# Batch 0 of an FNet and GLU kernel: the even slots of its sequence transform mixed by s mod 4 and summed over half the columns, the second weight piece merged last

## The chip, the cores and the metric

One Trainium2 chip, of which the kernel uses one core. The metric is the device time of one execution in microseconds: 1909.48 us, the median of three runs of the kernel before (1908.13 to 1910.03). The profile is one further execution of it.

## What is computed

The input x has 8 batches of 3008 rows of 256 numbers. Each batch goes through a Fourier transform over the rows and over the 256 features, of which the real part is kept; then every row goes through a gated feed-forward network (FFN).

```
X = np.fft.fft(x, axis=1); X = np.fft.fft(X, axis=2); x = X.real      # 8 x 3008 x 256
gate = 1 / (1 + exp(-(x @ w_gate)))                                   # 256 -> 1536
out  = (gate * (x @ w_val)) @ w_out                                   # 1536 -> 256
```

x is float32, the weights are float64.

## The kernel before

**Feature transform.** It is never computed on the data. Each piece of 256 columns of w_gate and w_val is multiplied by a small table `dt` (`merge`, L410: four matmuls into one PSUM bank, two copies on ScalarE into G2 and G1, two small DMAs into `ge`). A weight piece first has to be turned from float64 to float32: `weight_parts` (L377, two ScalarE instructions, L382 and L383), `weight_join` (L385, three VectorE instructions, L392 to L395, and one GpSimd addition, L397). Pieces are numbered by `jobs`: 0 is w_gate's first 256 columns, 1 is w_val's first, 2 and 3 the second ones, and so on. `weight_use(j)` calls `merge`. Below, "join j" and "merge j" are these steps of piece j.

**Sequence transform of batch 0.** The rows s = 0 to 767 stand as s = 6 p + q, partition p and slot q = 0 to 5, and with each come its mirror rows (3008 - s, 1504 + s, 1504 - s). VectorE folds these four (`half_rows`, L571, lines L494 to L583) into sums W for even frequencies (blk 0) and odd ones (blk 1). The folds go by `SLICES`: slots 0 and 1, slots 2 and 3, slot 4, slot 5. TensorE then multiplies the folds with the tables ST[0] (cosine) and ST[1] (sine), six slots each with 377 columns for even frequencies and 376 for odd ones. Even slots add up in one PSUM bank (`ev`), odd slots in another (`od`), because the first sum is symmetric and the second antisymmetric about the middle frequency: `places` (L611) makes the low frequencies from their sum (L613) and the high ones from their difference (L617), into pk (cosine) and qk (sine). These are 24 products of 377 or 376 columns, in four groups (two frequency blocks, cosine and sine).

**The e group.** One feature (number 128) has its own sums, twelve matmuls with one column of weights against the cosine table (`e_sums`, L696, tile `pe`), then copies on ScalarE (L720, L721, L726) and `places` on VectorE into `er`. The first 252 of them are copied into `e0`, which the FFN's first five groups multiply by G2; the whole is stored to DRAM (`ed`, L733), from where later groups get it as rows `ek` (`e_rows`, L760), with which ScalarE fills (seeds) their PSUM banks (L772).

**Order.** The whole program is an order written by hand; each engine runs its instructions in that order. SP issues all loads in program order: first weight pieces 0 and 1, then rows and tables slot by slot, then the other weight pieces. After both first merges come folds and products, then the FFN in 576 steps i: for each of 8 batches 6 chunks of up to 252 frequencies, for each chunk 12 groups of 128 hidden features. Step i issues `front_a(i)` (pk times G1), ScalarE's doubling `part(i)` (L787), the gate of group i - 1 (sigmoids L801 and L815, VectorE L802, L814, L818), `front_b(i)` (qk times G2), and from i = 5 on the output product of group i - 5. In steps 0 to 12 the remaining pieces are joined and merged, `weight_use(2)` in step 0 and 3 and 5 in step 1. Three PSUM banks (tag x) go round for `pf`, the FFN's sums; five others (po0 to po4) are for outputs and, earlier, for transforms.

**Side work.** `at(i, f)` hangs work on step i. For batch 1 rows are rearranged through DRAM (`xr`, L155 to L168), table rows are reversed into `rtab` (L206), and at steps 17 and 18 sixteen quarter loads (L247) refill the place of ST[1] for the later batches. At steps 21 to 27 seven `e_load`s follow (L685), columns of 4 bytes for feature 128 of the other batches, whose sums (`e_joint`, step 40) use ST[0] as batch 0 had it. The tables that later batches use are made at steps 42 on.

Of the kernel before, what the change touches and what calls it, by code (L numbers as in the profile page):

```python
# [8 lines left out]
F32 = mybir.dt.float32  # L9
# [72 lines left out]
def kernel(  # L82
# [107 lines left out]

    def load_rows(q, n):
        nc.sync.dma_start(out=X[0][0:NP, :, q : q + n], in_=xf[0, :, :, q : q + n])  # L192

    def load_table(t, q, n, lo=0, hi=NE + NO):
        nc.sync.dma_start(out=ST[t][0:NP, q : q + n, lo:hi], in_=stab[:, t, q : q + n, lo:hi])

# [206 lines left out]
    def weight_use(j):  # L403
        w, c = jobs[j]
        if w == 2:
            WO[c] = WS.pop(j)
        else:
            merge(WS.pop(j), w, c, (4, 2, 3)[next(turns) % 3] if j > 1 else None)

    def merge(ws, g, c, other):  # L410
        cs = slice(c * WC, (c + 1) * WC)
        ps = bank("ps", other)
# [71 lines left out]

    SLICES = ((0, 1), (2, 3), (4,), (5,))

    def fold_ops(b, nq):
# [83 lines left out]
        else:  # L571

            def half_rows(q):
# [9 lines left out]
                nc.vector.memset(r[:, :, :, 0:1], 0.0)  # L583
            ops += [lambda q=q: half_rows(slice(q[0], q[-1] + 1)) for q in SLICES]
        for blk, (v, r) in enumerate(parts):
# [8 lines left out]

    def half(b, w, d, blk, sn, other=None):


        c0, n = ((0, NE), (NE, NO))[blk]
        ev, od = [bank(name, other and other[i])[:, 0:n] for i, name in enumerate(("ev", "od"))]

        def sums(*qs):
            for q in sorted(qs, key=lambda q: q % 2):
                mm((ev, od)[q % 2], w(q), ST[int(sn)][0:NP, q, c0 : c0 + n], q < 2, q >= NQ - 2)

        def then():
            a = evp.tile([P, NE], F32, name="a", tag="a")[:, 0:n]
            nc.scalar.copy(a, ev)
            return lambda: places(d, blk, sn, a, od)
        return sums, then

# [68 lines left out]

    def seq_group(b, blk, what, other=None):  # L680
        return half(b, lambda q: W[b, blk][what][:, q, :], PQE[b][what], blk, what == 1, other)


    def e_load(b):
# [11 lines left out]
    def e_sums(m=B - 1):  # L696


        ps = bank("pe", NB - 1)
        at_ = lambda blk, par: slice((2 * blk + par) * TB, (2 * blk + par) * TB + m)  # L700
# [253 lines left out]
    load_x(0)  # L954
    for j in range(2):
        weight_load(j)
    load_rows(0, 2)
    load_table(0, 0, 2)
    load_rows(2, 2)
    load_table(1, 0, 2, 0, NE)  # L960
    load_table(0, 2, 2)
    load_rows(4, 1)
    load_table(0, 4, 1)
    load_rows(5, 1)
    weight_load(2)
    load_table(1, 2, 2, 0, NE)
    load_table(0, 5, 1)
    load_table(1, 4, 2, 0, NE)
    load_table(1, 0, NQ, NE)
    for j in (3, 5, 6, 8, 9, 4, 7):  # L970
        weight_load(j)
# [3 lines left out]
    weight_parts(0)  # L975
    weight_parts(1)
    weight_join(0)
    weight_join(1)
# [5 lines left out]
    seq_start(0)  # L984

    cos = [seq_group(0, blk, 0, (2 * blk, 2 * blk + 1)) for blk in range(2)]
    e_, e_even = e_sums(1)
    sin = [seq_group(0, 0, 1)]
    for q, f in zip(SLICES, fold_ops(0, 2), strict=True):
        f()  # L990
        e_(*{1: (0, 1), 5: (2, 3, 4, 5)}.get(q[-1], ()))
        sin[0][0](*{5: (3,)}.get(q[-1], ()))
        cos[0][0](*q)
        cos[1][0](*q)
        sin[0][0](*{1: (0, 1), 4: (2,), 5: (4, 5)}.get(q[-1], ()))
    places_c = [cos[blk][1]() for blk in range(2)]
    weight_parts(2)
    weight_join(2)
    rest, *ends = e_even()
    rest()  # L1000
    for f in ends:
        f()
    for f in places_c:
        f()
    nc.scalar.copy(e0[0:1], E0[0][:, 0:CH])
    weight_parts(3)
    weight_join(3)
    sin.append(seq_group(0, 1, 1, (0, 1)))
    sin[1][0](*range(NQ))
    for j in range(KEEP, KEEP + 3):  # L1010
        weight_load(j)
    places_s = [group[1]() for group in sin]
    for f in places_s:
        f()
    e_rows(0)
# [4 lines left out]
    def at(i, *fs):  # L1020
        side.setdefault(i, []).extend(fs)
# [21 lines left out]
    for i, f in zip((1, 2, 2, 2, 3, 4, 4, 4, 5, 6, 6, 8, 8, 8, 9, 9, 9, 9, 10, 10, 10, 11, 11), quarter_x(1), strict=True):  # L1043
        at(i, f)
    at(i0 + 1, lambda: load_x(1))
    for b in range(1, B):
        at(20 + b, lambda b=b: e_load(b))
# [198 lines left out]
```

## Time and profile before

| | |
|---|---|
| median of three runs | 1909.48 us |
| the profiled execution | 1909.15 us |
| its span, first to last instruction | 1907.4 us |
| TensorE busy | 1895.6 us, 99% |
| VectorE, ScalarE, GpSimd busy | 80%, 71%, 81% |
| granted TensorE clock | 1.00 throughout |
| first fold's last instruction | 15.40 us |
| ScalarE's first copy of batch 0's e sums starts | 26.18 us |
| first FFN matmul's weights loaded | 32.73 us |
| DMA, first 40 us | 290, 380, 381, 340 GB/s in tens of us |

In the lines of the profile, PE is TensorE's matmul, PEld its weight load, DVE VectorE, ACT ScalarE, POOL GpSimd, SPq the queue of SyncE that issues DMAs. A row of the timeline has the start in us, the duration in us, engine, line, operation, output and inputs, and in brackets how long the engine was idle before and what released it. A row of waits has who waited for whom, the total in us, how often, and the longest. A float32 matmul shows as two records. A row of the chain has start and duration of a piece of what ended last. A row of the stretches has a window, its length, the busy time (and instruction count) of PE, PEld, DVE, ACT and POOL, the clock, the DMA engines' busy share and GB/s.

### The profile page before, as it was taken

Reading aid. Unit: us, or ns where it says so; the run is one execution under the profiler, and the core shown is the slowest. Engines: PE = TensorE matmul, PEld = TensorE weight load, DVE = VectorE, ACT = ScalarE, POOL = GpSimd, SP = SyncE. Lnnn points to the kernel's source line nnn. Section 1 sums busy time; section 2 is a strip of 40 time slices with the busy share of each in tenths; the row PEclk is TensorE's granted clock in tenths of the full one; section 3 lists DMA queues with packets and bytes.
Section 4 is the critical chain, followed back from the end, with each engine's and each line's share of the span. In section 5 each row is a group of like instructions: output and inputs, shape, how many; then the busy total and the mean of one; then the engine's idle time right before and its main releaser. Section 6 shows DMA issues by size and latency. Waiting matters only on the chain.

```text
span 1907.4 us, 36057 instructions
## 1 busy us (share of the span) xinstructions
PE 1895.6 (99%) x11836; PEld 1756.6 (92%) x11836; DVE 1520.6 (80%) x3375; ACT 1353.2 (71%) x3235; POOL 1543.4 (81%) x2733
## 2 busy tenths in 40 slices
PE   8999999999999999999999999999999999999999
PEld 5788999999999999999999999999999999999998
DVE  7678888878979778897788878888788777977775
ACT  4777777777777777777777777677767777777775
POOL 2489879987999779997799878999789986877770
PEclk9999999999999999999999999999999999999999
DMA  8446221212022121211211212122120110010001
GB/s 315 120 134 80 71 89 51 72 33 81 21 64 54 31 87 32 62 41 37 89 39 48 45 39 81 40 52 58 30 74 17 36 37 15 15 25 17 15 18 30
DMA packets 197333, 109.33 MB, mean 57 GB/s; under 512 B 134823, under 2 KB 188818, under 8 KB 195354
## 3 DMA queue, kind: packets, MB, share of 16 engines
q1 hardware_dynamic: 196568, 106.50, 21.1%
q8 instruction: 95, 1.56, 0.3%
q14 instruction: 92, 0.75, 0.1%
q10 hardware_dynamic: 546, 0.51, 0.1%
q0 software_dynamic: 32, 0.00, 0.0%
HBM read 71.24 MB, written 47.87 MB: 62 GB/s over the span
## 4 chain that ended last, share of the span: by engine, by line
PE 94%; DMA 2%; SPq 1%; POOL 1%; ACT 1%; DVE 0%; issue 0%; ACTq 0%; POOLq 0%
PE pf L133 49%; PE po L133 41%; PE sum L133 2%; DMA rtab<-in_stab_dram 1%; PE ps L133 1%; POOL sf L824 1%; DMA st<-in_stab_dram 1%; SPq L206 1%; DMA raw<-in_moe_w_val_dram 0%; PE od L133 0%; POOL x L507 0%; SPq L192 0%; SPq L375 0%; PE pe L133 0%; PE ev L133 0%
## 5 line engine op out<-in xcount | busy, mean ns | idle before, releaser
L824 POOL TENSOR_TENSOR sf<-h,sf 128x168 f32<-128x168 f32 (+1 forms) x1104 | 621.0, 582 | 79.5 <-DVE h L818 75.9
L824 POOL TENSOR_TENSOR sf<-h 128x168 f32<-128x168 f32 (+1 forms) x920 | 519.3, 584 | 159.8 <-DVE h L818 158.0
L133 PE MATMUL pf<-qk,G 128*128 128x252 f32 (+1 forms) x2304 | 583.4, 376 | 0.9 <-ACT ae L787 0.8
L133 PE MATMUL pf<-pk,G 128*128 128x252 f32 (+1 forms) x2304 | 582.7, 376 | 0.0
L772 ACT ACTIVATE pf<-ek,ge 128x252 f32<-128x252 f32 (+1 forms) x1142 | 538.2, 471 | 23.2 <-DMA ge<-G 3.0
L133 PE MATMUL po<-sf,wf 128*128 128x168 f32 (+1 forms) x2944 | 508.3, 305 | 0.0
L787 ACT ACTIVATE ae<-pf 128x504 f32<-128x504 f32 (+1 forms) x576 | 338.8, 588 | 218.7 <-PE pf L133 217.2
L133 PEld LDWEIGHTS pf<-pk,G 128*128 128x128 f32 x2304 | 435.9, 190 | 53.3 <-ACT pf L772 1.5
L133 PE MATMUL po<-h,wf 128*128 128x168 f32 (+2 forms) x2584 | 461.3, 307 | 0.0
L133 PEld LDWEIGHTS po<-sf,wf 128*128 128x128 f32 x2944 | 453.4, 190 | 8.0
L818 DVE TENSOR_TENSOR h<-pf,z 128x252 f32<-128x252 f32 (+1 forms) x576 | 240.4, 417 | 274.0 <-ACT pf L815 270.5
L802 DVE TENSOR_TENSOR z<-ae,pf 128x504 f32<-128x504 f32 (+1 forms) x576 | 384.6, 668 | 83.1 <-ACT h L801 79.1
L908 DVE TENSOR_TENSOR c<-c 128x168 f32<-128x168 f32 (+1 forms) x920 | 438.7, 500 | 3.3
L133 PEld LDWEIGHTS pf<-qk,G 128*128 128x128 f32 x2304 | 410.6, 190 | 32.3 <-ACT ae L787 2.1
L133 PEld LDWEIGHTS po<-h,wf 128*128 128x128 f32 x2584 | 410.4, 190 | 17.8 <-issue 0.9
L801 ACT ACTIVATE h<-pf 128x252 f32<-128x252 f32 (+1 forms) x576 | 216.9, 376 | 146.3 <-PE pf L133 129.0
L815 ACT ACTIVATE pf<-z 128x252 f32<-128x252 f32 (+1 forms) x576 | 214.3, 372 | 116.4 <-DVE h L814 114.5
L814 DVE TENSOR_TENSOR h<-h,pf 128x252 f32<-128x252 f32 (+1 forms) x576 | 232.9, 404 | 0.0
L824 POOL TENSOR_TENSOR sf<-sf 128x168 f32<-128x168 f32 (+1 forms) x184 | 101.7, 553 | 14.4
L824 POOL TENSOR_TENSOR sf<-sf,h 128x168 f32<-128x168 f32 (+1 forms) x184 | 110.1, 598 | 0.0
L891 ACT COPY c<-po 128x504 f32<-128x504 f32 (+1 forms) x138 | 78.5, 569 | 0.0
L918 DVE STREAM_TRANSPOSE os<-c 128x256 f32<-128x256 f32 x188 | 76.5, 427 | 0.1
(158 smaller groups left out, 876.4 us busy)
## 6 DMA issues: line engine op xcount, KB each, us to landing
x<-xr SPq DMA_DIRECT2D x14, 1536.0 KB
out_dram<-os SPq DMA_DIRECT2D x376, 56.0 KB
xr<-in_xf_dram SPq DMA_DIRECT2D x105, 128.0 KB
x<-x SPq DMA_DIRECT2D x112, 96.0 KB
xr<-in_xf_dram SPq DMA_DIRECT2D x14, 384.0 KB
ek<-ed SPq DMA_DIRECT2D x40, 126.0 KB
out_dram<-os SPq DMA_DIRECT2D x288, 7.0 KB
xr<-in_xf_dram SPq DMA_DIRECT2D x21, 124.0 KB
```

What stands on the lines that cost most here:

```text
L133: nc.tensor.matmul(o, l, r, start=start, stop=stop, skip_group_check=True)
L772: nc.scalar.activation(PF[i][:, g], EK[i // NFT], AF.Copy, scale=ge[:, g, f : f + 1])
L787: nc.scalar.activation(AP[i], PF[i], AF.Copy, scale=2.0)
L801: nc.scalar.activation(H[p][:, fh, 0:n], PF[i][:, 0], AF.Sigmoid)
L802: nc.vector.tensor_tensor(z[:, :, ::-1], AP.pop(i), PF[i], op=ALU.subtract)
L814: nc.vector.tensor_tensor(h[:, fh, 0:n], h[:, fh, 0:n], pf[:, 1], op=ALU.mult)
L815: nc.scalar.activation(pf[:, 0], z[:, 0], AF.Sigmoid)
L818: nc.vector.tensor_tensor(h[:, fh, n:], pf[:, 0], z[:, 1], op=ALU.mult)
L824: nc.gpsimd.tensor_tensor(block(p, dst), block(p, a), block(p, b), op=(ALU.subtract, ALU.add)[op])
L891: (nc.vector.tensor_copy if t == 1 or t == 3 else nc.scalar.copy)(C[0][:, 3 * t * R : 3 * (t + 1) * R], PO[t][:, 0 : 3 * R])
L908: nc.vector.tensor_tensor(t[:, dst * R : (dst + 1) * R], *v, op=(ALU.subtract, ALU.add)[op])
L918: nc.vector.transpose(os_[0][0][:, s, 0:nb, h, :], t[:, c0 : c0 + nb * TB])
```

## The change

It concerns batch 0 and its loads, and adds two loads later.

- In slots 0 and 2 the even partitions and the odd partitions are exchanged between the two slots at loading (`mixed`), for rows and tables, so that slot 0 holds rows s = 0 mod 4 and slot 2 rows s = 2 mod 4. The sums of each have a symmetry of their own about the quarter frequency, so that only columns H0 to H1 (188 to 565, the upper half of the even frequencies and the lower half of the odd ones) are multiplied, into banks x and y.
- Slot 4 is not mixed at loading; its two kinds stand on alternate partitions. Its half columns are loaded into four tiles `apart` with zeros on the other kind's partitions (GpSimd memsets), so that its products are four, two for each bank.
- `copy` (ScalarE) and `join` (two VectorE instructions) make the full row of 753 even-slot sums from x and y; `places` then works from that row and the `od` banks.
- Order: rows and tables 1 and 3 are loaded first, weight piece 1 after rows 5; the cosine table's other columns of slots 0 and 2, in eight loads to alternate partitions, and slot 4 whole come after both slots 5, for the e group. `SLICES` becomes (1, 3), (0, 2), 4, 5. Merge 1 stands behind the e group; VectorE, not ScalarE, copies e0; the combinations for low frequencies (`pk(blk, 0)`, `qk(blk, 0)`) come first and those for high ones last, around the joins of pieces 2 and 3. The bank of the e group is one of the three of tag x.
- At step 20, `load_again` loads slots 0 and 2 of the cosine table unmixed, for `e_joint`.

```diff
+    def mixed(q):
+        return ((slice(0, NP, 2), q), (slice(1, NP, 2), 2 - q)) if q in (0, 2) else ((slice(0, NP), q),)
+    def load_rows(*qs):
+        for q in qs:
+            for ps, r in mixed(q):
+                nc.sync.dma_start(out=X[0][ps, :, q], in_=xf[0, ps, :, r])
+    H0, H1 = NE // 2, NE + NO // 2
+    def load_table(t, q, lo=0, hi=NE + NO):
+        for ps, r in mixed(q):
+            nc.sync.dma_start(out=ST[t][ps, q, lo:hi], in_=stab[ps, t, r, lo:hi])
+    apart = [[wf[:, 2 * t + h].rearrange("p m n -> p (m n)")[:, 6 * WC : 6 * WC + NE] for h in range(2)]
+             for t in range(2)]
+    def load_apart(t):
+        for h in range(2):
+            nc.sync.dma_start(out=apart[t][h][h:NP:2], in_=stab[h::2, t, 4, H0:H1])
+    def load_again():
+        for q in (0, 2):
+            nc.sync.dma_start(out=ST[0][0:NP, q], in_=stab[:, 0, q])
...
-            merge(WS.pop(j), w, c, (4, 2, 3)[next(turns) % 3] if j > 1 else None)
+            merge(WS.pop(j), w, c, HELD.pop(j) if j in HELD else bank("ps", 2 + next(turns) % 3 if j else None))
...
-    SLICES = ((0, 1), (2, 3), (4,), (5,))
+    SLICES = (slice(1, 4, 2), slice(0, 3, 2), slice(4, 5), slice(5, 6))
...
+    def seq_sums(what, x, y, od):
...
+        cols = (H0, NE - H0, 0), (NE, NO // 2, NE - H0)
+        def even(*qs):
+            for q in qs:
+                for blk, (lo, n, to) in enumerate(cols):
+                    for h in range(2):
+                        if q == 4 or h == q // 2:
+                            tab = apart[what][h][0:NP, to : to + n] if q == 4 else ST[what][0:NP, q, lo : lo + n]
+                            mm((x, y)[h][:, to : to + n], w[blk][:, q], tab, q != 4 and blk == 0, q == 4)
+        def odd(blk, *qs):
+            lo, n = ((0, NE), (NE, NO))[blk]
+            for q in qs:
+                mm(od[blk][:, 0:n], w[blk][:, q], ST[what][0:NP, q, lo : lo + n], q == 1, q == NQ - 1)
+        def copy():
+            a = evp.tile([P, NE], F32, name="a", tag="a")
+            nc.scalar.copy(a, y[:, 0:NE])
+            return a
+        def join(a):
+            f = hp.tile([P, 6 * WC], F32, name="u", tag="h") if what else wf[:, 0].rearrange("p m n -> p (m n)")
+            nc.vector.tensor_tensor(f[:, H0:H1], x[:, 0:NE], a, op=ALU.add)
...
+            nc.vector.tensor_tensor(f[:, 0 : 2 * H1].rearrange("p (b n) -> p b n", b=2)[:, :, H0 - 1 :: -1], *two,
+                                    op=ALU.subtract)
+            return lambda blk, *ends: places(d, blk, what == 1, f[:, blk * NE : NE + blk * NO],
+                                             od[blk][:, 0 : NE - blk], ends)
...
-        ps = bank("pe", NB - 1)
+        ps = bank("pe", NB - 1 if m > 1 else None)
...
+    for t in apart:
+        for tab in t:
+            nc.gpsimd.memset(tab, 0.0)
+    weight_load(0)
+    load_rows(1, 3)
+    for q in (1, 3):
+        load_table(0, q)
     load_rows(0, 2)
+    for q in (1, 3):
+        load_table(1, q)
+    load_rows(4)
+    for q in (0, 2):
+        load_table(0, q, H0, H1)
+    load_apart(0)
+    load_rows(5)
+    for q in (0, 2):
+        load_table(1, q, H0, H1)
+    load_apart(1)
+    weight_load(1)
+    for t in range(2):
+        load_table(t, 5)
+    for q in (0, 2):
+        load_table(0, q, 0, H0)
+        load_table(0, q, H1)
+    load_table(0, 4)
+    for j in (2, 3, 5, 6, 8, 9, 4, 7):
         weight_load(j)
...
+    next(folds)()
+    odd(0, 1, 3)
+    odd(1, 1, 3)
+    odd_s(0, 1, 3)
+    e_(1, 3)
+    next(folds)()
+    even(0, 2)
+    next(folds)()
+    even(4)
+    a = copy()
+    next(folds)()
+    pk = join(a)
+    HELD[1] = bank("ps")
+    od_s.append(bank("od"))
+    even_s(0, 2)
+    odd_s(1, 1, 3)
+    even_s(4)
+    odd(0, 5)
+    odd(1, 5)
+    weight_parts(1)
+    a = copy_s()
+    weight_join(1)
+    for blk in range(2):
+        pk(blk, 0)
+    qk = join_s(a)
+    odd_s(0, 5)
+    e_(0, 2, 4, 5)
+    qk(0, 0)
+    rest, last, end = e_even()
+    rest()
     weight_use(1)
+    odd_s(1, 5)
+    last()
+    nc.vector.tensor_copy(e0[0:1], E0[0][:, 0:CH])
     weight_parts(2)
+    qk(1, 0)
     weight_join(2)
+    qk(1, 1)
     weight_parts(3)
     weight_join(3)
+    for blk in range(2):
+        pk(blk, 1)
+    qk(0, 1)
+    end()
     for j in range(KEEP, KEEP + 3):
         weight_load(j)
...
+    at(20, load_again)
```

More of the change, by code (lines that the diff above doesn't have):

```diff
@@ L189 @@
     ed = dram.tile([B, NK + 1], F32, name="ed")
[L191 to L195, printed above, removed]
+    def mixed(q):
[16 more added lines that the diff above has]
+            nc.sync.dma_start(out=ST[0][0:NP, q], in_=stab[:, 0, q])
     NQ4 = NE // 4 + 1
@@ L407, in weight_use, with merge @@
         else:
-            merge(WS.pop(j), w, c, (4, 2, 3)[next(turns) % 3] if j > 1 else None)
-    def merge(ws, g, c, other):
+            merge(WS.pop(j), w, c, HELD.pop(j) if j in HELD else bank("ps", 2 + next(turns) % 3 if j else None))
+    HELD = {}
+    def merge(ws, g, c, ps):
         cs = slice(c * WC, (c + 1) * WC)
-        ps = bank("ps", other)
         for h in range(2):
@@ L583, in half_rows @@
                 nc.vector.memset(r[:, :, :, 0:1], 0.0)
-            ops += [lambda q=q: half_rows(slice(q[0], q[-1] + 1)) for q in SLICES]
+            ops += [lambda q=q: half_rows(q) for q in SLICES]
         for blk, (v, r) in enumerate(parts):
@@ L593 @@
     PQE = {}
[L595 to L609, printed above, removed]
+    def seq_sums(what, x, y, od):
+        d = PQE[0][what]
+        w = [W[0, blk][what] for blk in range(2)]
+        cols = (H0, NE - H0, 0), (NE, NO // 2, NE - H0)
[17 more added lines that the diff above has]
+            nc.vector.tensor_tensor(f[:, H0:H1], x[:, 0:NE], a, op=ALU.add)
+            two = [t[:, 1:NE].rearrange("p (b n) -> p b n", b=2) for t in (x, a)]
+            if what:
+                two.reverse()
+            nc.vector.tensor_tensor(f[:, 0 : 2 * H1].rearrange("p (b n) -> p b n", b=2)[:, :, H0 - 1 :: -1], *two,
+                                    op=ALU.subtract)
+            return lambda blk, *ends: places(d, blk, what == 1, f[:, blk * NE : NE + blk * NO],
+                                             od[blk][:, 0 : NE - blk], ends)
+        return even, odd, copy, join
     def places(d, blk, sn, ev, od, ends=(0, 1)):
@@ L678, in seq_start @@
             nc.vector.memset(t[:, NK:], 0.0)
-    def seq_group(b, blk, what, other=None):
-        return half(b, lambda q: W[b, blk][what][:, q, :], PQE[b][what], blk, what == 1, other)
     def e_load(b):
@@ L954 @@
     load_x(0)
-    for j in range(2):
-        weight_load(j)
-    load_rows(0, 2)
[L958 to L970, printed above, removed]
+    for t in apart:
[5 more added lines that the diff above has]
+        load_table(0, q)
+    load_rows(0, 2)
+    for q in (1, 3):
[16 more added lines that the diff above has]
+    for j in (2, 3, 5, 6, 8, 9, 4, 7):
         weight_load(j)
@@ L975 @@
     weight_parts(0)
-    weight_parts(1)
     weight_join(0)
-    weight_join(1)
     warm = bank("warm", 2)
@@ L982 @@
     weight_use(0)
-    weight_use(1)
[L984 to L996, printed above, removed]
+    seq_start(0)
+    folds = iter(fold_ops(0, 2))
+    even, odd, copy, join = seq_sums(0, bank("u"), bank("u"), [bank("od", t) for t in range(2)])
+    e_, e_even = e_sums(1)
+    od_s = [bank("od", 4)]
+    even_s, odd_s, copy_s, join_s = seq_sums(1, bank("u", 2), bank("u", 3), od_s)
+    next(folds)()
[28 more added lines that the diff above has]
+    rest()
+    weight_use(1)
+    odd_s(1, 5)
+    last()
+    nc.vector.tensor_copy(e0[0:1], E0[0][:, 0:CH])
     weight_parts(2)
+    qk(1, 0)
     weight_join(2)
[L999 to L1005, printed above, removed]
+    qk(1, 1)
     weight_parts(3)
     weight_join(3)
-    sin.append(seq_group(0, 1, 1, (0, 1)))
-    sin[1][0](*range(NQ))
+    for blk in range(2):
+        pk(blk, 1)
+    qk(0, 1)
+    end()
     for j in range(KEEP, KEEP + 3):
         weight_load(j)
-    places_s = [group[1]() for group in sin]
-    for f in places_s:
-        f()
     e_rows(0)
```

## The prediction

> **What bounds the kernel now.** I read the busy shares first, then the waits of TensorE, then the chain that ended last, piece by piece over the first 160 us, and then each engine's rows in order of time there. The first line says that TensorE is busy almost from end to end; the next three are all that it waits for after its first 6 us.
>
> ```profile
> PE 1895.6 (99%) x11836; PEld 1756.6 (92%) x11836; DVE 1520.6 (80%) x3375; ACT 1353.2 (71%) x3235; POOL 1543.4 (81%) x2733
> ...
> PE ps L133 <- POOL raw L397: 1.6, 1, 1.6
> PE pf L133 <- ACT ae L787: 0.8, 2, 0.6
> PE ev L133 <- DVE x L583: 0.2, 1, 0.2
> ```
>
> So from about 33 us on, where the FFN's first matmuls begin, the time is TensorE's own work, which the diff leaves alone. What can change is when that stream starts, whether it then runs without holes, and two added transfers near 146 us. The chain shows what sets the start: transfers until 23.7 us, then TensorE alone.
>
> ```profile
> 14.43 9.31 DMA st<-in_stab_dram
> 23.74 0.04 issue
> 23.78 0.90 PE ev L133 x2
> 24.68 1.37 PE pe L133 x16
> ...
> 33.21 4.25 PE pf L133 x20
> ```
>
> The stretches give the transfer rate that my sum uses: 2.9 MB in the first 10 us, then 0.38 MB/us (last column, GB/s).
>
> ```profile
> 0.00:10.00 10.00, 4.21 (x13) 3.50 (x14) 3.64 (x6) 3.94 (x6) 2.80 (x8) 1.00 0.83 290
> 10.00:20.00 10.00, 8.19 (x34) 4.58 (x33) 9.72 (x18) 1.29 (x4) 2.15 (x1) 1.00 1.04 380
> 20.00:30.00 10.00, 9.90 (x43) 4.92 (x42) 8.20 (x23) 3.91 (x8) 1.28 (x1) 1.00 1.06 381
> ```
>
> Check: up to cosine slot 5 the old order moves 8.07 MB, due at 10 + 5.17/0.38 = 23.6 us; it landed at 23.7.
>
> **Transfers, part by part.** Sizes: a row slot 0.52 MB, a table slot 0.386, a weight piece 0.52. What must have landed before the last small e matmul is in the new order 8.70 MB (both tables' odd slots and slots 5, the cosine table whole, half columns of sine slots 0 and 2, the four "apart" halves of slot 4 with 0.097 MB each, weight pieces 0 and 1). By volume: rows 1 and 3 at 7.4 us, the mixed rows at 12.0, rows 4 at 15.4, rows 5 at 18.3, weight piece 1 at 21.2, cosine slot 5 at 22.2, sine slot 5 at 23.2, cosine slot 4 at 25.3. Rows land about 0.6 to 1.1 us after their volume (rows 5 of before: by volume 20.2, seen at 21.3).
>
> The count of issues matters too. The issue of piece 3 at 18.83 waited 1.1 us for rows 4, eight issues back, and that of piece 6 at 21.35 waited 0.2 us for rows 5, again eight back: at most eight are under way. The new list puts eight pieces of 48 KB (columns outside the half range, by even and odd partitions) ahead of cosine slot 4. Eight such pieces are 0.385 MB, 1 us of traffic, while an issue takes some 0.45 us (the 16 quarter loads at L247 go out every 0.47) and its data about 2 us more. So slot 4 is issued only when the first of the eight has landed, near 24.6, and lands near 27.7 instead of 25.6.
>
> Here a rule of the Trainium skill speaks against the change: "DMA: Bandwidth & Descriptors", Bandwidth, says that transfers under 64 KB are dominated by descriptors and lists 0.95 us for 64 KB. Eight at that price would be 7.6 us against my 3.6, and slot 4 would land 4 us later than I say; the smallest pieces this trace shows in a stream, the 141 KB quarter loads, do not reach down to that size.
>
> **VectorE's folds.** Now join 0 and join 1 come first (5.72 to 10.2) and the first fold ends at 15.4 (5.2 us, with 1.1 us lost while GpSimd's add holds it: L498 shows 1.25 us against 0.16 later). After, only join 0 stands ahead (to 7.3); rows 3 land near 8.0, GpSimd's add runs until 8.8, then 4.1 us as the second fold has now (15.38 to 19.49): 12.9, so 2.5 us earlier. Second fold 17.2 (rows by 13.1), third 19.7, fourth 22.2 (2.5 each, as now).
>
> **TensorE's sums.** A 377-column product costs 0.63 us in the rows (16.56 to 17.19). One of 188 or 189 columns is not in the trace. Bounds: 0.31 by columns, 0.38 if its two weight loads of 190 ns bind; the 168-column products run at 1.43 us for five (0.286 each), so I take 0.32. Sixteen of them cost 5.1 us (6.1 at the other bound) where twelve wide ones cost 7.6: 2.5 us (1.5) of TensorE time saved. In order after 12.9: six odd products 3.8, four e matmuls 0.8 (to 17.5), four halves 1.3, a wait for the third fold to 19.8, four halves 1.3 (21.1), four more 1.3, two odd 1.25, four halves 1.3 (24.9), three with slot 5 1.9 (26.8), then eight e matmuls 1.4, which wait at slot 4: end about 28.4, against 26.05 now. So the sums as a whole end earlier, but the e group ends later: 6.7 us of sine products stand behind it now (26.05 to 32.73) and cover its chain, and only 2.4 us after (merge 1 and two products).
>
> **Behind the e group.** From its end the trace has two copies on ScalarE, two combinations on VectorE, a copy, a combination and the copy of e0:
>
> ```profile
> 26.18 0.47 ACT L720 COPY z<-pe 1x377 f32<-1x377 f32 x1 [0.82 <-PE pe L133]
> 26.65 0.47 ACT L721 COPY z<-pe 1x376 f32<-1x376 f32 x1
> ...
> 28.18 0.47 ACT L726 COPY ae<-pe 1x376 f32<-1x376 f32 x1 [1.06 <-DVE er L617]
> 29.31 0.40 ACT L1005 COPY wqk<-er 1x252 f32<-1x252 f32 x1 [0.66 <-DVE er L613]
> ```
>
> 3.66 us from 26.05 to 29.71. After: e0 at 28.4 + 3.66 = 32.1. Meanwhile TensorE does merge 1 (1.73) and two sine products (0.63) to 30.8, and the bank of the e sums, which pf 0 now takes, comes free at 31.0. So the first FFN group starts at 31.0 (now 32.7), waits for G1's copy and e0, and ends at 33.0; the second ends at 34.7, merge 2 starts at 35.6 (now 37.1). So far 1.5 us are gained.
>
> Then VectorE is late. Its queue is in order, and what stands behind the e combinations is longer than now: last 0.5, e0 0.4 (moved from ScalarE), qk 0.5, join 2 1.55, qk 0.5, join 3 2.1 (0.6 of it blocked by GpSimd's add, as L393 of 1.41 at 38.12 is now), three late combinations 1.5, the last of e 0.5, join 5 1.55. From 28.4 + 2.8 that ends at 40.4. Now it ends at 37.74, after an idle 1.27:
>
> ```profile
> 36.13 0.43 DVE L392 TENSOR_SCALAR wqk<-wqk 128x512 f32<-128x512 f32 x1 [1.27 <-ACT wqk L382]
> 36.59 0.43 DVE L393 TENSOR_SCALAR wqk<-wqk 128x512 int32<-128x512 int32 x1
> 37.05 0.69 DVE L395 SCALAR_TENSOR_TENSOR wqk<-raw,wqk 128x512 int32<-128x512 int32 x1
> ...
> 38.12 1.41 DVE L393 TENSOR_SCALAR wf<-wf 128x512 int32<-128x512 int32 x1
> ```
>
> GpSimd's 1.3 us add makes piece 5 ready at 41.8, and merge 5 needs it: 41.9 against 41.65 now. Merge 3 waits 0.8 on the way and the gain is spent. Join 6 and gate 0 follow 2.8 us later than now on VectorE, so ScalarE's sigmoids and the doubling for group 2 end at 47.2 and the matmul on them starts at 47.3 against 46.80: **0.5 us lost**. From there ScalarE and VectorE idle 0.9 to 2.7 us in each step of now (L802 waits 0.86, 1.48, 2.67), so they catch up in two or three steps. The sum moves one for one with the end of the e group: no change at 27.9.
>
> **The two reloads** (0.77 MB) stand in SP's queue between the quarter loads and the e loads:
>
> ```profile
> 146.53 11.06 SPq L685 DMA_DIRECT2D x<-in_xf_dram  x5
> 157.69 1.88 SPq L760 DMA_DIRECT2D ek<-ed  x1
> 163.25 0.98 ACT L772 ACTIVATE pf<-ek,ge 128x252 f32<-128x252 f32 x2 [0.30 <-DMA ek<-ed]
> ```
>
> The row ek that is queued behind five e loads is already 0.3 us late for ScalarE. Two issues of 0.45 make it 1.2; the matmul that needs the seed comes some 0.6 us after its usual start, so TensorE loses about 0.3. Bounds: nothing, if the e loads (2 us each, transfer share 0.55 to 0.9) take it up, and 1.5, if the whole 0.77 MB at 0.36 MB/us (2.1 us) stands ahead. The rest of the chain there (xr, rtab, quarter loads, with the 0.6 us wait at 147.8) hangs on merge 13's copy at 76.7 and moves with TensorE: no term. The four memsets (about 0.5 each by the 0.34 of 252 columns) lie between 2 and 4 us, where GpSimd is idle.
>
> **The sum.** 1909.15 (span 1907.4 and 1.75 outside it) + 0.5 + 0.3 = 1909.95; the median of the runs is 1909.48, 0.33 above the profiled one. I forecast 1910.1.
>
> **Rivals.** *The early start survives.* If GpSimd's adds hold VectorE less than I count (0.8 us of the first fold, 0.6 of join 3) and cosine slot 4 is not late, the e group ends at 27.4 and join 5 some 1.6 us earlier; then the 1.5 us by which merge 2 is early are kept in part or whole, with the 1 us of the e group at most 2.2: 1907.0 to 1908.8. For it: TensorE's work shrinks and the folds begin earlier. Against it: VectorE's in-order queue.
> *Half-partition transfers are slow.* 2.6 MB of the new list go to 64 alternate partitions. The quarter loads, to 32 partitions, moved at 214 GB/s (140 to 145 us) where full ones reach 380. At that rate 2.6 MB take 12.1 us instead of 6.8, the e group ends near 33.7, and the kernel is 5.5 us slower: 1915. It decides from about 300 GB/s (8.7 us, 2 us slower). Against it: alternate partitions span the whole range, a quarter load only a fourth. The Trainium skill's "SBUF — State Buffer", Door 1, has bandwidth follow the ports that the partitions reach; by its table even partitions reach all of them, so by that page nothing would be lost.
> *The reload hurts.* All of its 2.1 us in front of ek: 1.5 us of TensorE instead of 0.3, 1911.3.
> *Half the columns don't halve the time*, with 0.38 us a product: one us more before the e group, 1911.
>
> **Chances.** Forecast, within about 1 us of 1910.1: 0.45. Early start: 0.22. Reload 0.12, narrow products 0.08, slow transfers 0.13. Two in ten left out of the range: it goes from 1907.3 (most of the early start) to 1913.5 (the reload and the narrow products together, a part of the slow transfers). What a measurement tells from no change is about 0.2%, 3.8 us. Faster by that needs more than the whole early start: 0.03. Slower by that needs the slow transfers, or two rivals at once: 0.13. Else the same: 0.84.
>
> **What the profile after would show.** First fold's end at 12.9, half products at 0.32 us, the second e group ending near 28.4 with a wait for the cosine table, first pf near 31.0, merge 2 near 35.6, merge 5 near 41.9 behind GpSimd's add, the third qk matmul group at 47.3; an ek wait near 1.2 us at some 163 us. A first fold after 14 us, an e group ended before 27 or after 30, or TensorE waiting where I have it busy would make this wrong.

## The result and the profile after

The changed kernel takes 1915.89 us (median of 6 runs, 1914.6 to 1917.3), the kernel before 1909.21 us (median of 6): ratio 1.0035, interval 1.0022 to 1.0048. It is slower by 6.7 us where 0.6 were forecast, and outside the range. The profiled execution took 1915.91 us with a span of 1914.1 us, 6.76 us more than before.

The page of the changed kernel and the waits of its TensorE (engine, tile and line that waited, what ended the wait, total us, times, longest us):

```profile
PE 1897.6 (99%) x11844; PEld 1758.0 (92%) x11844; DVE 1523.8 (80%) x3380; ACT 1351.6 (71%) x3232; POOL 1544.7 (81%) x2737
...
PE pf L133 <- ACT G L439: 1.7, 1, 1.7
PE ps L133 <- POOL wqk L417: 1.3, 2, 0.7
PE pe L133 <- DMA st<-in_stab_dram: 1.3, 1, 1.3
PE pf L133 <- ACT pf L810: 1.0, 1, 1.0
PE od L133 <- DVE x L604: 1.0, 1, 1.0
PE u L133 <- DVE x L604: 0.6, 1, 0.6
```

Where 2.6 us of waits stood after the first 6 us, these six alone make 6.9. One lies at 170 us (`pf` on L810), the others before 50 us. In the lines below, the chain that ended last runs through two of them, the first and the third of the list (start, duration, what ran): a table load and the e products behind it, then VectorE's queue, the gate, and two copies on ScalarE.

```profile
27.55 3.78 DMA st<-in_stab_dram
31.37 0.86 PE pe L133 x8
...
46.28 0.67 DVE z L840
46.95 0.34 DVE h L852
...
47.37 0.38 ACT pf L853
...
49.16 0.28 ACT G L439
...
49.48 0.69 PE pf L133 x2
```

The rows of the first fold's last instruction and of TensorE show the same places (start, duration, instruction, idle time before it and its releaser):

```profile
12.90 0.06 DVE L604 MEMSET x<- 128x4 f32 x1
...
20.49 1.54 PE L133 MATMUL u<-wf,x 128*128 128x189 f32 x8 [0.58 <-DVE x L604]
...
31.37 0.81 PE L133 MATMUL pe<-st,x 128*1 128x377 f32 x8 [1.28 <-DMA st<-in_stab_dram]
...
42.00 1.99 PE L133 MATMUL ps<-wqk,dt 128*128 128x256 f32 x8 [0.73 <-POOL wqk L417]
...
45.40 1.99 PE L133 MATMUL ps<-wqk,dt 128*128 128x256 f32 x8 [0.56 <-POOL wqk L417]
...
49.48 0.69 PE L133 MATMUL pf<-pk,G 128*128 128x252 f32 x2 [1.67 <-ACT G L439]
...
52.59 1.01 PE L133 MATMUL pf<-qk,G 128*128 128x252 f32 x4
```

The last row is the third group of qk matmuls, group 2's second half, forecast at 47.3; below it is **the mark**. In the kernel before it is this row:

```profile
46.80 1.01 PE L133 MATMUL pf<-qk,G 128*128 128x252 f32 x4
```

So 5.8 of the 6.76 us are lost ahead of it. The rest is found by subtraction: profiled time less mark is 1862.35 us before and 1863.32 us after, so 1.0 us is lost behind it.

### The profile page after: what moved, and what is told of

Read it like the earlier page. It is cut to its first block, busy times and chain, and to the rows that moved or that the text cites. A ratio compares the mean times of both kernels' runs of the same rounds, so it can differ in the third digit from the quotient of the medians.

```text
span 1914.1 us, 36121 instructions
## 1 busy us (share of the span) xinstructions
PE 1897.6 (99%) x11844; PEld 1758.0 (92%) x11844; DVE 1523.8 (80%) x3380; ACT 1351.6 (71%) x3232; POOL 1544.7 (81%) x2737
## 4 chain that ended last, share of the span: by engine, by line
PE 95%; DMA 2%; DVE 1%; POOL 1%; ACT 1%; SPq 0%; issue 0%; ACTq 0%; POOLq 0%
PE pf L133 50%; PE po L133 42%; PE sum L133 2%; DMA st<-in_stab_dram 1%; POOL sf L862 1%; PE ps L133 1%; DMA x<-in_xf_dram 0%; DMA ek<-ed 0%; POOL x L528 0%; SPq L204 0%; PE pe L133 0%; DVE c L946 0%; DVE z L840 0%; ACT pf L810 0%; ACT wl L496 0%
## 5 line engine op out<-in xcount | busy, mean ns | idle before, releaser
L810 ACT ACTIVATE pf<-ek,ge 128x252 f32<-128x252 f32 (+1 forms) x1142 | 538.3, 471 | 24.7 <-DMA ge<-G 3.1
L946 DVE TENSOR_TENSOR c<-c 128x168 f32<-128x168 f32 (+1 forms) x920 | 444.4, 507 | 3.3
```

The lines of the kernel that those rows point to most:

```text
L810: nc.scalar.activation(PF[i][:, g], EK[i // NFT], AF.Copy, scale=ge[:, g, f : f + 1])
L946: nc.vector.tensor_tensor(t[:, dst * R : (dst + 1) * R], *v, op=(ALU.subtract, ALU.add)[op])
```

## The experiments

Single edits move the medians by 1.4 to 1.9 us, no more than the half width of one interval, so each reading rests on the profile's marks as well. All runs are in this table, each ratio against the kernel before on the same chip; the runs come from several chips, so between groups (e1 to e4, e5 to e8, e9 to e12, e13 to e16, e17 and e18) the ratios compare and the medians only roughly. The columns: the end of the e group (last `pe` row), the mark, the profiled time less the mark, and the median with its ratio to the kernel before.

| kernel | e group ends | mark | mark less e end | behind the mark | median | ratio, interval |
|---|---|---|---|---|---|---|
| before | 26.05 | 46.80 | 20.75 | 1862.4 | 1909.2 | |
| after | 32.18 | 52.59 | 20.41 | 1863.3 | 1915.89 | 1.0035, 1.0022 to 1.0048 |
| e1 whole slots | 30.56 | 50.97 | 20.41 | 1863.0 | 1914.01 | 1.0028, 1.0018 to 1.0038 |
| e2 reload late | 33.25 | 53.66 | 20.41 | 1861.9 | 1914.47 | 1.0030, 1.0019 to 1.0042 |
| e3 before, halves | 25.88 | 46.63 | 20.75 | 1862.2 | 1909.59 | 1.0003, 0.9993 to 1.0012 |
| e4 order alone | 31.77 | 52.24 | 20.47 | 1861.9 | 1914.41 | 1.0030, 1.0018 to 1.0042 |
| e5 join 6 late | 32.21 | 50.64 | 18.43 | 1863.3 | 1914.06 | 1.0026, 1.0015 to 1.0037 |
| e6 e group early | 26.10 | 50.36 | 24.26 | 1865.3 | 1915.17 | 1.0031, 1.0019 to 1.0043 |
| e7 e6, late joins, late reload | 26.22 | 48.52 | 22.30 | 1864.7 | 1912.09 | 1.0017, 1.0008 to 1.0027 |
| e8 before, join 6 late | 25.56 | 46.31 | 20.75 | 1862.7 | 1909.40 | 1.0001, 0.9992 to 1.0011 |
| e9 e7, later combinations | 26.12 | 49.18 | 23.06 | 1863.3 | 1911.68 | 1.0012, 1.0002 to 1.0021 |
| e10 e1 + e2 + e5 | 30.45 | 48.88 | 18.43 | 1862.7 | 1911.07 | 1.0008, 0.9999 to 1.0018 |
| e11 before, piece 1 last | 26.85 | 51.34 | 24.49 | 1862.3 | 1912.86 | 1.0016, 1.0007 to 1.0026 |
| e12 e10, later combinations | 30.13 | 49.35 | 19.22 | 1863.2 | 1912.13 | 1.0014, 1.0005 to 1.0023 |
| e13 after, piece 1 first | 33.17 | 53.55 | 20.38 | 1864.3 | 1916.61 | 1.0041, 1.0026 to 1.0056 |
| e14 e10, piece 1 first | 31.03 | 49.44 | 18.41 | 1862.1 | 1912.36 | 1.0020, 1.0011 to 1.0030 |
| e15 e4, piece 1 first | 33.48 | 53.94 | 20.46 | 1862.3 | 1916.36 | 1.0040, 1.0025 to 1.0055 |
| e16 e11, four more products | 27.65 | 52.85 | 25.20 | 1864.0 | 1915.23 | 1.0032, 1.0019 to 1.0044 |
| e17 e10, e products paired | 30.12 | 48.61 | 18.49 | 1861.9 | 1910.94 | 1.0012, 1.0003 to 1.0022 |
| e18 after, e products paired | 32.32 | 52.74 | 20.42 | 1863.9 | 1916.52 | 1.0038, 1.0024 to 1.0052 |

In e2 nothing ahead of step 20 differs, yet its mark is 1.1 us later than the changed kernel's: that much a start-up varies from one execution to the next. (There TensorE waits 1.14 us for slot 5 of the table, 0.23 us in the changed kernel.)

**Are half-partition transfers slow (e3), or the many small ones (e1)?** e3 is the kernel before with every load of rows and tables of batch 0 as two, by even and odd partitions; e1 (second diff) is the changed kernel without the eight small loads.

```diff
...
-        nc.sync.dma_start(out=ST[t][0:NP, q : q + n, lo:hi], in_=stab[:, t, q : q + n, lo:hi])
+        for h in range(2):
+            nc.sync.dma_start(out=ST[t][h:NP:2, q : q + n, lo:hi], in_=stab[h::2, t, q : q + n, lo:hi])
```
```diff
-        load_table(0, q, H0, H1)
+        load_table(0, q)
...
-    for q in (0, 2):
-        load_table(0, q, 0, H0)
-        load_table(0, q, H1)
```

> The kernel before, with each of its early loads of rows and tables of batch 0 (not of weights) cut into one load for even and one for odd partitions. Theory H: 7.8 MB at some 20 to 40% less, the first FFN matmul 3 to 6 us later, 1912 to 1915. Theory S: the pieces are still 190 KB to 0.5 MB, whose issue at 0.63 us is hidden behind their transfer; 1909 to 1910, first FFN matmul at 32.5 to 33.5.

> Slots 0 and 2 of the cosine table are loaded whole and mixed before the apart halves (four loads of 192 KB instead of four of 96 KB), and the eight 48 KB loads ahead of cosine slot 4 are gone. Volume and the share of half-partition transfers stay the same. Theory S (each small piece costs SP some 0.63 us of issue, so 48 to 96 KB pieces starve the transfers): slot 4 lands near 28 instead of 31.3, the e group ends near 28.7 instead of 32.2, and the kernel comes to 1912 to 1913. Theory H (transfers to alternate partitions are slow in themselves): slot 4 still lands after 30.5 and the kernel stays at 1915 to 1916.

e3 changed nothing measurable: for halves of 0.19 MB and more the rate holds. e1 took the 1.28 us wait away and moved e end and mark 1.6 us forward, between the two forecasts. The trace shows a slow queue on SP. In the changed kernel (start, duration, line, issue, how many) its eleven issues up to slot 4 follow one another every 0.6 us with no wait shown, while whole-partition ones come every 0.5. Then come the stretches (last two columns, the DMA engines' busy share and GB/s; 380 before), and the chain there:

```profile
21.50 6.64 SPq L204 DMA_DIRECT2D st<-in_stab_dram  x11
28.18 0.43 SPq L395 DMA_DIRECT2D raw<-in_moe_w_gate_dram  x1
28.65 0.47 SPq L395 DMA_DIRECT2D raw<-in_moe_w_val_dram  x1
```
```profile
26.00:28.00 2.00, 1.91 (x6) 1.06 (x6) 1.93 (x5) 0.61 (x2) 0.53 (x1) 1.00 0.74 190
28.00:30.00 2.00, 2.00 (x9) 0.37 (x8) 1.81 (x5) 0.00 (x0) 0.76 (x1) 1.00 0.74 154
```
```profile
22.00 4.98 DMA st<-in_stab_dram
...
26.99 0.51 SPq L204
...
27.55 3.78 DMA st<-in_stab_dram
```

The chain has one landing in it, at 26.97, which the issue at 26.99 waited for; but the issue before that one began at 26.27 and so ended only some 0.1 us earlier. So issuing alone brings slot 4 to nearly the same time. e13, below, confirms it: its chain there has no landing, only issues of 0.59 us end to end from 23.95 on, until slot 4's at 28.42. A second cause is not separated from this: the DMA engines are 0.74 busy in those stretches and move half or less of what they move at 1.04, so the small pieces cost them more per byte too.

**The new wait for G (e5).** Join 6 goes behind gate 0; e8 is the same edit in the kernel before.

```diff
-        (pre if j in (5, 6) else join).setdefault(0 if j == 6 else i, []).append(lambda j=j: weight_join(j))
+        (pre if j == 5 else join).setdefault(i, []).append(lambda j=j: weight_join(j))
```

> The changed kernel with one line moved: join 6 (three VectorE instructions, 2.4 us with its blocked one) goes from ahead of gate 0 into gate 0, beside join 8. Theory G: the 1.7 us for which TensorE waits at the second matmul of group 2 comes from ScalarE's queue, where merge 3's copies stand behind gate 0's sigmoid, which stands behind VectorE's joins 5 and 6; with join 6 out of the way that wait goes or shrinks below 0.5 us and the kernel comes to 1914.0 to 1914.8. Rival: VectorE has the same work in the same stretch, merge 6 is late instead, and the kernel stays at 1915.5 to 1916.

> The kernel before with the one line of e5. There TensorE has no wait between 33 and 146 us, so nothing is to be gained: 1908.5 to 1909.5. Tells whether e7's gain, if any, is the mixing's or this line's.

In e5 the 1.7 us wait is gone and the stretch from e end to mark falls from 20.41 to 18.43; in the kernel before the edit does nothing (20.75 both times), since there TensorE has its own sums to do. The chain was: merge 3's copies stand in ScalarE's queue behind gate 0's second sigmoid, which waited 4.33 us for VectorE, which had joins 5 and 6 ahead of gate 0. ScalarE's rows in the changed kernel:

```profile
47.37 0.38 ACT L853 ACTIVATE pf<-z 128x252 f32<-128x252 f32 x1 [4.33 <-DVE h L852]
...
49.05 0.38 ACT L439 COPY G<-ps 128x256 f32<-128x256 f32 x1
```

**The reload (e2)** goes from step 20 to 28.

> The changed kernel with its two reloads at step 28, behind all seven e loads and the row ek, instead of step 20. If the reload costs TensorE what its wait for L810 shows, that wait of 1.0 us goes and the kernel comes to 1914.8; ScalarE waits 0.6 us or less for ek. Rival: the e loads alone, 6 us later than before against TensorE's steps, hold ek back anyway, and the kernel stays at 1915.5 to 1916.

TensorE's wait on L810 and ScalarE's for `ek` are gone, and the stretch behind the mark is 1.4 us shorter, where 1.0 was expected. In the changed kernel the five e loads and `ek` stand behind the two reloads on SP, and ScalarE's seeding waits for it:

```profile
150.93 1.08 SPq L215 DMA_DIRECT2D st<-in_stab_dram  x2
152.24 11.07 SPq L723 DMA_DIRECT2D x<-in_xf_dram  x5
163.41 1.81 SPq L798 DMA_DIRECT2D ek<-ed  x1
...
169.68 0.98 ACT L810 ACTIVATE pf<-ek,ge 128x252 f32<-128x252 f32 x2 [1.65 <-DMA ek<-ed]
```

**The order alone (e4)**: slots 0, 2 and 4 as before the change (no mixing, no `apart`, full products, no reload), all else in the new order. Slot 4 comes whole where its halves stood, and ScalarE copies the even sums instead of VectorE joining them.

> The new order of loads, folds, sums and merges, but nothing mixed: slots 0, 2 and 4 loaded whole over all partitions, even sums over all columns in twelve wide products, no reload. Tells what the order alone does. 17 issues fewer, 0.4 MB more and 2.5 us more of products: by theory S the e group ends near 30.1 and the kernel comes to 1912.5 to 1913.5, faster than the changed one although the sums are longer. If the order were neutral and the mixing the whole loss: 1909 to 1910.

By its ratio e4 is 5.7 us slower than before, more than either forecast, so the order by itself costs nearly all that the change costs. Its transfers run at full rate (393 GB/s from 20 to 30 us, 229 in the changed kernel) and its e group still ends at 31.77, on TensorE's products. The changed kernel saves 2.4 us of these and then waits for slot 4.

**The e group early (e6), with late joins and reload (e7), with later combinations (e9).** e6 loads slots 0 and 2 of the cosine table whole as pairs, moves its slots 4 and 5 ahead of the sine loads, and the e products up behind each cosine slot.

```diff
     even(4)
     a = copy()
+    e_(0, 2)
     next(folds)()
...
+    odd(0, 5)
+    odd(1, 5)
+    e_(4, 5)
...
-    e_(0, 2, 4, 5)
```

> The changed kernel with the e group taken forward: cosine slots 0 and 2 whole and mixed in two loads, slots 5 and 4 of the cosine table and weight piece 1 ahead of the sine table's halves, the e matmuls with each fold, their end before the sine sums, which then cover their chain. Mixing and half columns stay. In before, changed kernel, e1 and e4 alike group 2's second half starts 20.4 to 20.8 us after the e group's end. If the place of the e group is the loss (theory E), its end comes to 24.5 to 26 us, group 2's second half to 46 to 47.5, and the kernel to 1909.5 to 1911 (with the reload's 0.9). If VectorE's longer queue is the loss wherever the e group stands: 1912 or more.

> e6 with join 6 inside gate 0 (as e5) and the reload at step 28 (as e2). If the three causes are separate and add up: 0.9 less than e6 by the reload and 0 to 1.5 less by join 6, 1907.5 to 1909.5. If they hide each other: the same as e6.

> As e7 (e group early, joins 5 and 6 late; 1912.1 us), with the combinations of the cosine places that nobody needs soon, the end of the e sums and the copy of e rows moved from ahead of gate 0 to steps 1 to 3, and the join of the two column halves written forwards, from reversed inputs, so that its write does not overlap the tile that a late transfer still fills. By the theory that VectorE's in-order queue between the fourth fold and gate 0 sets the start of the FFN stream, group 2's second half comes about 1.5 us earlier than in e7 (47.0 instead of 48.52) and the time is 1910.3 to 1911.0. By the rival, that TensorE's own queue (the sine sums that stand behind) sets it, nothing is gained: 1911.8 to 1912.4.

The e group ended at 26.10, as before the change, yet e6's mark came only 2.2 us earlier: my theory that the e group's end alone sets the start fell. VectorE then works from 26.07 to gate 0 at 44.05 with one pause of 0.63 us, and a 1.84 us wait stands ahead of that:

```profile
26.07 0.55 DVE L651 TENSOR_TENSOR wf<-u,a 128x376 f32<-128x376 f32 x1 [1.84 <-DMA wf<-in_stab_dram]
26.54 0.42 DVE L416 TENSOR_SCALAR raw<-raw 128x512 f32<-128x512 f32 x1
...
44.05 0.67 DVE L844 TENSOR_TENSOR z<-ae,pf 128x504 f32<-128x504 f32 x1
```

e7 takes join 6 out of that queue, has the late reload too, and is 3.1 us faster than e6, yet far from the 1907.5 to 1909.5 expected. e9 takes three more combinations out and turns the join's writing direction; the wait of 1.8 us stayed, the mark did not move forward, and the combinations, now in steps 1 to 3, delay gate 1 there (ScalarE waits 2.22 us for `er`). Its 1911.68 us is within e7's scatter.

**All three edits (e10), and later combinations there (e12).**

> The changed kernel with three of the single edits together: slots 0 and 2 of the cosine table loaded whole, join 6 behind gate 0, and the reload eight steps later. If the three costs are apart from one another (1.9, 1.8 and 1.4 us by the single runs), the time is 1910.5 to 1911.5, group 2's second half near 49.0, and neither the wait for slot 4, nor that for the G copies, nor that for ek is left. If whole slots and the late join gain the same microseconds (both shorten what stands ahead of the same matmul), 1912 to 1913.

> As e10, with the two late combinations of the cosine places, the end of the e sums and the copy of the e rows moved from ahead of gate 0 to steps 1 to 3. By the theory of VectorE's queue some 1.0 to 1.5 us of its work leaves the path, group 2's second half comes about 1 us earlier than in e10 and the time is 0.7 to 1.5 us less than e10's: 1909.3 to 1910.5. By the rival, that with e10's edits TensorE's sums set the start: the same as e10 within 0.3 us.

e10: 1911.07 us, as the sum of three separate costs (1.9 + 1.8 + 1.4) says, and its interval lies wholly below the changed kernel's: together the three costs are shown. All three waits are gone; what TensorE waits for is

```profile
PE od L133 <- DVE x L604: 1.3, 1, 1.3
PE ps L133 <- POOL wqk L417: 1.2, 2, 0.7
PE od L133 <- DMA st<-in_stab_dram: 0.5, 1, 0.5
PE u L133 <- DVE x L604: 0.5, 1, 0.5
PE pf L133 <- ACT ae L825: 0.4, 2, 0.2
```

Its mark is still 2.1 us later than before the change, though its ratio (0.9999 to 1.0018) no longer tells it from the kernel before. e12 missed both its forecasts: it is 1.1 us slower than e10. Like e9 it shows that what leaves the queue ahead of gate 0 comes back as a wait one step later (ScalarE waits 2.23 us for `er`).

**Weight piece 1 last, alone (e11), and undone (e13, e14, e15).** The diff is e11's, of the kernel before; the other three are its reverse in the changed kernel, e10 and e4.

```diff
-    for j in range(2):
-        weight_load(j)
+    weight_load(0)
...
     load_rows(5, 1)
+    weight_load(1)
     weight_load(2)
...
     sin[1][0](*range(NQ))
+    weight_use(1)
```

> The kernel before with only the third part of the change: weight piece 1 loaded behind the last rows, its join behind the fourth fold and its merge last. By the theory of VectorE's queue a join of 1.5 to 2.2 us moves from ahead of the folds, where VectorE had to wait for rows anyway, to behind them: the first fold ends 2 us earlier, but the sums are still led by transfers, the e group ends within 0.5 us of before, and the FFN's stream starts 1 to 3 us later: 1910.0 to 1912.0. By the rival, that the place of this piece does not matter and the loss of the changed kernel is all in the order of its sums: 1909.0 to 1909.8.

> The changed kernel with its third part undone: weight piece 1 loaded behind piece 0, its join ahead of the folds and its merge ahead of the sums, as before. First theory (a merge and a join moved out of time in which TensorE and VectorE wait for rows anyway): the first fold ends near 15.4 again instead of 12.9, yet the stretch from the e group's end to the FFN's first matmul loses the 1.7 us merge and VectorE's queue ahead of gate 0 loses a join of 1.8 us: the e group ends near 32.4, the first FFN matmul starts at 33.2 instead of 34.8, and the time is 1912.5 to 1914.3. Rival (the sums' order alone is at fault and starting them 2.5 us later costs what the merge gives): 1915.3 to 1916.5.

> The same undoing in the kernel with the three edits (1911.07 us: whole slots, late join 6, late reload). First theory: the sums start 2.4 us later, the merge of 1.7 us and a join of 1.8 us leave the path: the first FFN matmul starts near 32.6 instead of 33.05, VectorE reaches gate 0 some 1 to 2 us earlier, 1909.3 to 1910.6. Rival (TensorE's late start binds): 1911.0 to 1912.0. Below 1909.0, faster than before, only if the 2.4 us of narrower products come through as well.

> The same undoing in the kernel with the new order alone, unmixed and with full products (1914.41 us). First theory: 1911.9 to 1913.5, and what is then left above the time before is the order of the sums and of VectorE's queue alone. Rival, as above: 1914.0 to 1914.8.

Alone, the part costs the kernel before 3.4 us. Its sums are led by transfers (slot tables until 23.9 us), so the earlier folds gain nothing; merge 1 leaves an idle stretch of TensorE for the end of a queue that is full, and a 2.1 us pause opens, after which the granted clock is low in some executions (below). I took from this that undoing it would help the changed kernel. It does not: the ratios of e13, e14 and e15 are 0.0006, 0.0012 and 0.0010 above those of their kernels (1.1, 2.3 and 1.9 us, each within the intervals), and their marks are 1.0, 0.6 and 1.7 us later. Their sums start over 2 us later and the e group ends 0.6 to 1.7 us later; the stretch to the mark stays 20.4 and 18.4. Merge 1 was never on that stretch: it covers the e group's chain of copies, and without it TensorE waits there (1.8 us for e0 in e13). The same part is a loss in one order and, as far as the marks tell, a small gain in the other.

**Four more products (e16).** Meant to fill e11's pause.

```diff
+        if q[-1] == 5:
+            HELD[jobs[1]] = bank("ps")
+            for i in range(4):
+                mm(HELD[jobs[1]][:, 0:WC], dt[:, 0, 0:P], dt[:, 0], True, True)
```

> The kernel before with weight piece 1 last (1912.86 us; there TensorE waits 2.1 us for a table slot at 22 us, and from 25 to 29 us its granted clock is 0.5 to 0.75), with four products of the warm-up kind added just ahead of that wait, into the bank that the late merge overwrites. If the pause brings the low clock, it is gone, the e products are back at 1.4 us for sixteen records, and the time is 1911.0 to 1911.9. If the low clock comes from something else, it stays, and with it 1912.4 to 1913.4.

The experiment missed its aim. The pause belongs to a product one step earlier (sine slot 2), so the four stood behind it, at 28.32. Pause and low clock stayed. The mark came 1.5 us later, about the 1.7 us of the added products, since TensorE's queue is full there; the ratio rose by 3 us, from 1.0016 to 1.0032. What the pause does to the clock was not tried in any other way.

**The e products in pairs (e17 in e10, e18 in after).**

```diff
-    e_(1, 3)
...
-    e_(0, 2, 4, 5)
+    e_(1, 0, 3, 2, 5, 4)
```

> The kernel with the three edits (1911.07 us; its e group ends at 30.4), with the e products in pairs of an odd and an even slot, (1, 0), (3, 2), (5, 4), all in the last e group, instead of odd slots early and even ones late. Theory: the four sums (block by parity of the slot) stand in four column groups of TensorE and run at once when four of them are neighbours, as in the kernel before (eight records in 0.7 us); slots of one parity use two groups and take twice as long (eight records in 1.36 us at 17.0). The first e group and its 1.4 us go away and the last still takes 2.0 us: the e group ends near 29.1, group 2's second half comes near 47.5, 1909.5 to 1910.0. Rival, if VectorE's or the folds' times bind and not TensorE's: 1910.7 to 1911.5.

> The changed kernel with only the e products in pairs. If slot 4 of the cosine table, which lands at 31.3, is what the last e group ends on, the 1.4 us that TensorE saves are hidden in the wait for it: the e group still ends near 32.1 and the time is 1915.5 to 1916.3. If TensorE's own work sets the end of the group: 1914.2 to 1914.8.

The weight loads (PEld: start, duration, count) show the theory's first half: four at a time in the kernel before, two at a time in the changed one, where the slots have one parity; the third fence has TensorE's rows of e17.

```profile
24.93 0.10 PEld L133 LDWEIGHTS pe<-st,x 128*1 128x1 f32 x4 [0.21 <-issue]
25.25 0.10 PEld L133 LDWEIGHTS pe<-st,x 128*1 128x1 f32 x4 [0.21 <-issue]
```
```profile
17.32 0.09 PEld L133 LDWEIGHTS pe<-st,x 128*1 128x1 f32 x2 [0.23 <-issue]
17.63 0.09 PEld L133 LDWEIGHTS pe<-st,x 128*1 128x1 f32 x2 [0.23 <-issue]
```
```profile
18.56 1.68 PE L133 MATMUL u<-st,x 128*128 128x189 f32 x8 [1.25 <-DMA st<-in_stab_dram]
...
28.04 2.08 PE L133 MATMUL pe<-st,x 128*1 128x377 f32 x24
```

All 24 records now take the 2.0 us that 16 took. But the 1.4 us saved at 17 us came back as the wait of 1.25 us in its first row: transfers and folds lead TensorE there. The e group ended 0.33 us sooner, and the times are those of e10 and after within the intervals. For e18, slot 4 covers it, as its first forecast said; for e17 the rival held. No version tried beats the kernel before.

## Why the prediction was wrong, point by point

The sum was 1909.15 + 0.5 + 0.3. Three of its steps failed: the landing of cosine slot 4 with the end of the e group, the path behind the e group, and the size of the reload.

- **Cosine slot 4 (failed, with the e group's end: 32.18 instead of 28.4, 3.8 us).** "An issue takes some 0.45 us", taken from loads to 32 neighbouring partitions, was wrong for these: 0.6 us. And SP was held by issuing at least as much as by transfers under way: slot 4 was issued at 27.55 instead of 24.6 and landed at 31.33 instead of 27.7. e1 puts some 1.6 us of the 3.8 on it (start-ups differ by up to 1.1 us). The rule of the Trainium skill that I weighed and did not take ("DMA: Bandwidth & Descriptors", Bandwidth) would have had slot 4 land 4 us later, at 31.7: its landing came true, but not its price: the eight pieces went out in 5.1 us (22.46 to 27.55), not in 7.6. The rows of 0.47 us an issue were no bound for a kind of load that they did not show.
- **The sums ahead of it (the other 2.2 us).** The first fold ended at 12.90 as forecast, half products took 0.32 us as forecast (eight records 1.28 us apart). But the second fold ended at 17.9, the third at 20.4, the fourth at 22.9, each 0.7 us late; and four e products of one parity took 1.36 us instead of 0.8, the last eight 2.0 (e1, e10) instead of 1.4, because I took their time from rows where four ran at once. e17 shows that the first of these was covered by folds and transfers; that the second counts in full no run shows by itself. The tables' slots 5, due by volume at 22.2 and 23.2, were late too: in e1 and e10 the chain has SP's issues end to end from 17 us, then slot 5, which lands near 26.2, and TensorE's products behind it.
- **Behind the e group (failed: 20.41 instead of 18.9, 1.5 us).** I followed VectorE's queue, and there the figures hold: merge 3 waits 0.73 us (forecast 0.8), merge 5 starts 13.2 us behind the e group (13.5). I did not follow ScalarE's: G copies of merge 3 behind a sigmoid that waits for that same VectorE queue, and a pk matmul behind the copies, which waits 1.67 us. e5 measures 2.0 us.
- **The reload (failed in size: 1.0 instead of 0.3 us).** The mechanism was right, ScalarE's wait 1.65 us instead of 1.2; what TensorE loses of it is 1.03 us. e2: 1.4 us.
- **Sum of the misses**: mark 52.59 instead of 47.3, 5.3 us, plus 0.7 behind it: 1909.95 + 6.0 = 1915.95, against 1915.91. That it closes proves nothing, since mark and rest are parts of one trace; that the three waits are separate costs is what e10 shows.
- **"The sum moves one for one with the end of the e group; no change at 27.9."** The first half is right in the order as changed: seven kernels with join 6 early have 20.4 us to the mark, whatever else differs, four with it late 18.4. "No change" would have needed 26.4. And with the e group moved up (e6) the rule ends, and VectorE's queue, with one pause of 0.63 us from 26.07 to gate 0, is then as late by itself.
- **Rivals.** Slow half-partition transfers gave 1915, close to the result by luck, by a mechanism that e3 refutes; "Door 1" of "SBUF — State Buffer" in the Trainium skill, by which alternate partitions lose nothing, agrees with e3 (1.0003). The early start did not come. The reload was nearer to its rival (1.5 us) than to the forecast. Narrow products cost what was forecast.

What stays open: e10's mark is 2.1 us later than before, though its products are 2.4 us shorter. The runs show what does not explain it (merge 1's place, the e products' pairing, combinations ahead of gate 0), and that its e group ends 4.4 us later. Two paths set the start of that group within half a microsecond of each other. In e10 the chain has slot 5's landing (issued at 21.43) and the three products behind it:

```profile
21.43 4.74 DMA st<-in_stab_dram
...
26.31 2.14 PE od L133 x6
```

In e17, where the first e products are gone, it has the second fold, the third and TensorE's products, and the group starts at 28.04 instead of 28.38. What either would be worth was not tried.

## What to carry to other kernels

TensorE is full here, and a chain of small steps ends in its next stream. Moving that chain to the back cost more than the shorter products gave: the kernel before had 6.7 us of other products behind the e group, which cover such delays (join 6's place costs it nothing, e8). Follow every in-order queue that the chain crosses, ScalarE's as well as VectorE's. Splitting a load multiplies issues: count them at the time of an issue of that very shape, and put a small late load behind what is needed first.

## What the runs showed of the hardware

- **After a pause of 2.1 us the granted clock fell.** In e11 TensorE waits 2.09 us until 23.95; from 25 us on its granted clock (the last column but two) is 0.73 and then half or little more, until 29 us; three products that take 2.17 us in the kernel before take 3.19 at 26.78. In e16 the same follows the same pause.

```profile
24.00:25.00 1.00, 1.00 (x6) 0.35 (x10) 0.97 (x3) 0.63 (x2) 0.28 (x1) 1.00 1.06 369
25.00:26.00 1.00, 1.00 (x14) 0.21 (x8) 1.00 (x1) 0.00 (x0) 1.00 (x1) 0.73 1.06 379
26.00:27.00 1.00, 1.00 (x9) 0.22 (x2) 0.96 (x2) 0.04 (x1) 0.08 (x1) 0.50 1.07 385
27.00:28.00 1.00, 1.00 (x2) 0.62 (x3) 0.15 (x3) 0.89 (x2) 0.78 (x1) 0.50 1.07 386
28.00:29.00 1.00, 1.00 (x3) 0.51 (x2) 0.93 (x2) 0.04 (x1) 0.50 (x1) 0.56 1.05 390
```

  The pauses of 1.28 and 1.67 us in the changed kernel left the clock at 1.00, and so did one of 2.10 us in e17, at 11 to 13 us; its length alone does not decide. The Trainium skill ("TensorE: Matmul & The Clock Gate", Part 1) has the clock halved after at least one idle window of about 3.4 us, the windows running freely. These two traces do not agree with that length, since the pause ahead of the low clock is 2.09 us; the windows themselves show in no run here. That the pause brings the low clock was not shown by an edit (e16). e11's times also scatter most: five of its ten executions have a mean clock of 0.999 (1913.1 to 1914.7 us), the other five 1.000 (1910.8 to 1912.6 us), so the low clock came in about half of them, which are some 1.8 us longer by their medians.
- **Products with one column of weights ran four at once**, with records 0.09 us apart that last 0.48 us each, where their outputs lie 32 partitions apart in four places, and two at once (0.17 us) where neighbours use two places. The Trainium skill's "TensorE: Matmul & The Clock Gate", Part 3, describes such products running at once; the trace agrees on that, though its records start 0.09 us apart where the page has about 4 ns.
